# Gate logits in one bank spread by small copies, waits named in a new order, weight loads in paced parts

## The chip, the cores and the metric

One core of a Trainium2 chip. The metric is the device time of one execution in microseconds (us). In these traces PE runs the matmuls (9886 records in the kernel before), ACT the activations (729), DVE and POOL elementwise work (1073 and 626 records), and SP issues 147 of the 151 plain copies. The program gives each engine its own list; where one instruction had to wait, those behind it waited too (POOL in run c1, for 7.0 us).

## The reference, cut to what matters

S = 2048 rows, D = 512, 32 heads of 16. A softmax attention (A) and a linear attention (B) are mixed by a gate per row.

```python
g = sigmoid((x * gate_w).sum(-1, keepdims=True))
a = softmax((q @ k.T) * 16 ** -0.5) @ v @ A_wo            # per head, q, k, v from x @ A_wqkv
b = (phi(q) @ (phi(k).T @ v)) / (phi(q) @ sum(phi(k))) @ B_wo  # q, k, v from x @ B_wqkv
return g * a + (1 - g) * b
```

## The kernel before

A program on the host schedules every instruction of every engine ahead of time. A "round" is one query chunk of 512 rows with half of the heads of one group; there are 32, of about 20 us each. In a round PE makes score blocks. ACT exponentiates pairs of them (695 in all, 128x1024), the path "P". DVE and POOL do the other 658 blocks by integer arithmetic, the path "Z". PE then multiplies both with the values.

Every instruction gets a list of waits on the semaphores of other engines, and they are issued in list order:

```python
    def add(self, fn, deps=(), inc=True, dma_sem=None):
        waits = []
        for d in deps:                       # in the order of the operands
            ...
            for k, (s2, v2) in enumerate(waits):
                if s2 is sem:
                    if val > v2:
                        waits[k] = (sem, val)
                    break
            else:
                waits.append((sem, val))
...
        def emit_engine(E, eng):
            for waits, fn, inc, dma_sem in E.ops:
                for sem, val in waits:
                    eng.wait_ge(sem, val)
                h = fn()
```

The gate's sigmoid is spread over partitions by DVE copies, and each weight matrix is one load:

```python
        def t_gate():
            ...
            for qc in range(NQC):                      # four times: 16 matmuls, a transpose, a copy
                b = yield ("BANK",)
                ... 
                yield dv(607, lambda b=b: nc.vector.transpose(gl, bank(b)), [r_bank[b]], [r_gl])
                yield po(250, lambda qc=qc: nc.gpsimd.tensor_copy(ge[:, qc, :], ...), [r_gl], [r_ge])
            ...                                        # exp on ACT, +1 on POOL, reciprocal on DVE, 1-g on POOL
            for a in range(4):
                yield dv(150, lambda a=a, src=src: nc.vector.tensor_copy(gnat[32 * a:32 * (a + 1), :], src), [r_ge], [r_gnat])
...
        dma(SP, wA[:], wsrc, semWA, 16, 9000.0, writes=[r_wA, r_wAk], issue=500.0)      # 1536 KB
        def t_wb():
            yield ("DMA", wB[:], ..., semWB, 16, 12000.0, [], [r_wB], False, True)      # 1536 KB
```

The queries of each later chunk and group are written as `QT` and copied by eight SP copies into a zero-padded `Qz`, which the scores read:

```python
            for par in range(2):
                for j in range(4):
                    p0 = 32 * j + 16 * par
                    yield ("DMA", Qz[p0:p0 + 16, s, par, :], QT[p0:p0 + 16, a, :], semQ[s], tot, 2500.0, [r_QT[a]], [r_Qz[s][par]], False, j == 0)
```

The softmax here doesn't subtract the row's maximum and nothing guards it: scores larger than these inputs give would overflow.

## Time and profile before

| | before |
|---|---|
| median time of three runs | 681.13 us (680.4 to 681.41) |
| span of the profiled run | 679.8 us |
| ACT's first exponential starts | 10.67 us |
| ACT's last exponential starts | 670.36 us |
| from there to the end | 9.47 us |

ACT is the engine to watch, so I keep one account throughout. The time from one exponential's start to that of ACT's next activation is 904 ns when nothing holds it up, and 477 ns after one of the linear attention's 32 activations; these are the usual shortest steps in the trace. Whatever a step takes beyond them I call **lost**. As the exponentials don't change in number, the span is: start of the first, a fixed floor, the lost time, and the tail after the last. Before, 17.05 us are lost.

ACT's busy time by stretches in the kernel before (columns: stretch, its length, ACT's busy time and instruction count, clock of PE, share of the copy engines, GB/s):

```profile
20.00:40.00 20.00, 13.76 (x15) 0.91 0.45 161
40.00:60.00 20.00, 20.00 (x23) 1.00 0.06 15
60.00:669.00 609.00, 608.43 (x680) 1.00 0.06 15
```

### The profile page before, as it was taken

To read this page: it belongs to the slowest core of one execution; us is meant where nothing else is said; L and a number is where in the kernel's file an instruction comes from. 1 tells how busy PE (TensorE), PEld (TensorE's weight loads), DVE (VectorE), ACT (ScalarE), POOL (GpSimd) and SP (SyncE) were. 2 spreads that over 40 slices of the span, in tenths; PEclk is the share of its full clock that TensorE was granted. 3 is DMA by queue.
4 is the path that set the end of the run, shared out by engine and by line. 5 is a ranking of instruction groups with operands and counts; after the bars stand their busy time and mean duration, and the time that the engine had idled before them with its cause. 6 is when DMAs were issued, how large, how long until landed. Compare 5 with 4: busy or idle time off the path is not lost.

```text
span 679.8 us, 24140 instructions
## 1 busy us (share of the span) xinstructions
PE 664.7 (98%) x9886; PEld 203.6 (30%) x9910; DVE 605.1 (89%) x1073; ACT 658.2 (97%) x734; POOL 550.7 (81%) x626
## 2 busy tenths in 40 slices
PE   8899999999999999999999999999999999999997
PEld 3323232322222222322333322222233322222222
DVE  5789889989899998989899998898999998998995
ACT  5799999999999999999999999999999999999995
POOL 4669878898888888888878888878589888889883
PEclk9999999999999999999999999999999999999999
DMA  6500002100000000000000100000003220000000
GB/s 132 203 18 3 9 2 72 33 2 10 2 9 2 7 6 2 10 2 2 12 3 23 52 10 1 10 3 2 1 11 53 38 49 25 17 18 17 18 18 32
DMA packets 27869, 15.96 MB, mean 23 GB/s; under 512 B 19697, under 2 KB 26737, under 8 KB 27761
## 3 DMA queue, kind: packets, MB, share of 16 engines
q1 hardware_dynamic: 26416, 13.91, 8.0%
q8 instruction: 79, 1.29, 0.8%
q10 hardware_dynamic: 1344, 0.52, 0.3%
q14 instruction: 30, 0.24, 0.1%
HBM read 6.69 MB, written 2.10 MB: 13 GB/s over the span
## 4 chain that ended last, share of the span: by engine, by line
ACT 42%; PE 42%; issue 14%; DVE 1%; DMA 1%; ACTq 0%; POOL 0%; POOLq 0%
ACT P L756 41%; PE ps L363 32%; PE ps L369 9%; ACT eb L1029 1%; DMA xnat<-wA 1%; DVE Z L672 0%; PE ps L884 0%; ACTq L1433 0%; DVE wA L1135 0%; DVE Z L734 0%; DVE T L994 0%; ACT KT L906 0%; ACT wA L1174 0%; POOL warm L407 0%; ACT gt L980 0%
## 5 line engine op out<-in xcount | busy, mean ns | idle before, releaser
L756 ACT ACTIVATE P<-ps 128x1024 bf16<-128x1024 f32 x695 | 645.3, 1126 | 7.4 <-PE ps L363 7.4
L724 POOL TENSOR_TENSOR Z<-Z,mcon 128x512 int32<-128x512 int32 x464 | 477.7, 1054 | 77.6 <-DVE Z L672 46.1
L672 DVE TENSOR_SCALAR Z<-ps 128x512 int16<-128x512 f32 x658 | 441.9, 683 | 57.0 <-PE ps L363 49.8
L363 PE MATMUL ps<-Z,Vc 128*17 128x512 bf16 x1974 | 283.8, 383 | 0.2
L363 PE MATMUL ps<-Qz,KT 32*128 32x512 bf16 x2048 | 272.1, 385 | 4.0 <-ACT P L756 2.3
L363 PE MATMUL ps<-P,Vc 128*17 128x512 bf16 x1390 | 253.0, 383 | 0.0
L363 PEld LDWEIGHTS ps<-Qz,KT 32*128 32x128 bf16 x2048 | 67.9, 91 | 260.4 <-ACT P L756 237.8
L363 PEld LDWEIGHTS ps<-Z,Vc 128*17 128x17 bf16 x1974 | 64.4, 88 | 78.2 <-issue 50.7
L734 DVE TENSOR_SCALAR Z<-Z 128x1024 int16<-128x1024 int16 x194 | 79.8, 430 | 0.2
L363 PEld LDWEIGHTS ps<-P,Vc 128*17 128x17 bf16 x1390 | 57.5, 88 | 55.1 <-issue 42.9
L363 PE MATMUL ps<-warm 128*32 128x512 bf16 (+13 forms) x618 | 59.3, 330 | 4.5 <-issue 3.0
L369 PE MATMUL ps<-xT,wA 128*32 128x512 bf16 x512 | 42.9, 382 | 0.0
L1030 POOL TENSOR_SCALAR eb<-eb 128x512 f32<-128x512 f32 x32 | 19.9, 622 | 16.9 <-DVE Z L734 7.4
L961 POOL TENSOR_SCALAR Vc<-Vc 128x576 bf16<-128x576 bf16 x32 | 21.9, 685 | 8.0 <-DVE Vc L958 5.2
L1017 POOL TENSOR_TENSOR T<-T,rg 128x256 bf16<-128x256 f32 x31 | 19.6, 634 | 8.6 <-DVE Z L734 5.3
L363 PEld LDWEIGHTS ps<-warm 128*32 128x32 bf16 (+1 forms) x642 | 20.8, 95 | 17.5 <-issue 10.3
L994 DVE STREAM_TRANSPOSE T<-ps 128x512 f32<-128x512 f32 x32 | 22.7, 709 | 3.0 <-PE ps L363 2.9
L369 PE MATMUL ps<-wA,xT 128*32 128x128 bf16 x1024 | 22.1, 220 | 2.2 <-issue 2.2
L369 PE MATMUL ps<-wB,xT 128*32 128x512 bf16 x256 | 23.4, 382 | 0.0
L369 PE MATMUL ps<-wA,OAT 128*32 128x512 bf16 x256 | 23.0, 381 | 0.0
L369 PE MATMUL ps<-xT,wB 128*32 128x512 bf16 x256 | 22.4, 383 | 0.0
L369 PE MATMUL ps<-wA,xnat 128*32 128x512 bf16 x256 | 22.3, 381 | 0.0
(79 smaller groups left out, 283.4 us busy)
## 6 DMA issues: line engine op xcount, KB each, us to landing
Qz<-QT SPq DMA_DIRECT2D x120, 16.0 KB, 1.8
wA<-in_A_wqkv_dram SPq DMA_DIRECT2D x1, 1536.0 KB, 7.8
wB<-in_B_wqkv_dram SPq DMA_DIRECT2D x1, 1536.0 KB, 11.9
xnat<-in_A_x_dram SPq DMA_DIRECT2D x3, 512.0 KB, 5.3
out_dram<-outt SPq DMA_DIRECT2D x12, 128.0 KB, 1.7
wA<-in_A_wo_dram SPq DMA_DIRECT2D x1, 512.0 KB, 4.3
wA<-in_B_wo_dram SPq DMA_DIRECT2D x1, 512.0 KB, 5.2
out_dram<-wA SPq DMA_DIRECT2D x4, 128.0 KB, 1.8
```

The lines of the kernel that those rows point to most:

```text
L363: return lambda: nc.tensor.matmul(o, lhsT=l, rhs=r, start=start, stop=stop, skip_group_check=sg)
L369: h = nc.tensor.matmul(o[32 * j:32 * j + 32], lhsT=l[:, 32 * j:32 * j + 32], rhs=r, start=start, stop=stop, skip_group_check=True)
L672: return C(DV, 400, 533 * n + 74, lambda: nc.vector.tensor_scalar(o, i, ZB, 0.0, op0=ALU.add, op1=ALU.max), [r_bank[b] for b in bks], r_Z[ ...
L724: return C(PO, 400, 70 + 484 * n, lambda: nc.gpsimd.tensor_tensor(Z[:, z, 0:512 * n].bitcast(I32), Z[:, z0, 0:512 * n].bitcast(I32), mcon[ ...
L734: return C(DV, 450 if hot else 300, 69 + 134 * n, lambda: nc.vector.tensor_scalar(Z[:, z, 0:512 * n], Z[:, z0, 0:512 * n], float(m), None, ...
L756: return C(AC, 500, 427 * n + 49, lambda: nc.scalar.activation(P[:, slot, 0:512 * n], bank(b0, n), ACT.Exp, scale=ESC), [r_bank[b0 + k] fo ...
L961: yield po(690, lambda k=k: nc.gpsimd.tensor_scalar(Vc[:, k, vs].rearrange("p a b c -> p (a b c)"), Vc[:, 0, vs].rearrange("p a b c -> p ( ...
L994: yield dv(607, lambda: nc.vector.transpose(T1[:, a, :], bank(7)), [r_bank[7]], [r_T1[a]])
L1017: yield po(640, lambda: nc.gpsimd.tensor_tensor(t2[:, :, 16 * par:16 * par + 16], t1[:, :, 0:16], rg[:, a, :].unsqueeze(2).to_broadcast([1 ...
L1029: yield ac(480, lambda: nc.scalar.activation(eb[:, i, :], bank(b), ACT.Exp), [r_bank[b]], [r_eb[i]])
L1030: yield po(640, lambda: nc.gpsimd.tensor_scalar(eb[:, i, :], eb[:, i, :], 1.0 + 1e-6, 0.0, op0=ALU.min, op1=ALU.max), [r_eb[i]], [r_eb[i]])
```

## The change

The intent: let ACT start sooner, keep the heavy loads of the first 40 us apart, relieve DVE and PE of gate work, name the wait that is expected last at the end of the list, and shorten the tail. Besides, 18 instead of 16 buffers for Z and other constants of the scheduler. Cut to its core:

```diff
-        for d in deps:
-            if d is None:
-                continue
+        for d in sorted([d for d in deps if d is not None], key=lambda d: d.fin if isinstance(d, _Ev) else 0.0):
...
                 if s2 is sem:
-                    if val > v2:
-                        waits[k] = (sem, val)
+                    val = max(val, v2)
+                    del waits[k]
                     break
-            else:
-                waits.append((sem, val))
+            waits.append((sem, val))
...
-    FILL = 0.755
+    FILL = 0.7
-    NPS, NZ, NQZ, NVQ = 10, 16, 3, 8
+    NPS, NZ, NQZ, NVQ = 10, 18, 3, 8
...      # gate: logits of all four chunks in one bank, one transpose, one small exp and reciprocal, then
+                for a in range(4):
+                    yield ("DMA", gt[32 * a:32 * (a + 1), qc, :], ge[32 * qc:32 * (qc + 1), 0, :], semGN, 256, 2500.0, [r_ge], [r_gt], False,
+                           qc == 0 and a == 0)
+            yield po(200, lambda: nc.gpsimd.tensor_scalar(gp[:], gt[:].rearrange("p q (c a) -> p a (q c)", a=4), -1.0, 1.0, op0=ALU.mult, op1=ALU.add),
+                     [r_gt], [r_gp])
             for a in range(4):
-                yield dv(150, lambda a=a, src=src: nc.vector.tensor_copy(gnat[32 * a:32 * (a + 1), :], src), [r_ge], [r_gnat])
+                yield ("DMA", gnat[32 * a:32 * (a + 1), :], gp[32 * a:32 * (a + 1), a, :], semGP, 64, 2500.0, [r_gp], [r_gnat], False, a == 0)
...      # loads: each part waits for PE's latest instruction, so PE's progress paces it
+        def t_load(k, n, dst, src, sem, lat, wr, flag):
+            yield ("DMA", dst, src, sem, 16 * n, lat + 1000.0, [now()], wr, False, k == 0)
...
+            add_task(t_load(cc, NCC, wA[:, cc, :], wsrc[:, cc, :], semWA, 3500.0, [r_wA, r_wAk], "wa"), 0.3 + 0.15 * cc, 0.9, f"WA{cc}")
+            add_task(t_load(cc, NCC, wB[:, cc, :], wsrcB[:, cc, :], semWB, 3500.0, [r_wB], "wb"), 0.9 + 0.2 * cc, 1.8, f"WB{cc}")
...      # last round: transpose, reciprocal, products and transpose back in two halves of 256 columns
-            if tail and qbl % 2 == 1:
+            if tail and qbl != 2:
                 yield ac(480, lambda: nc.scalar.copy(ot, bank(b)), [r_bank[b]], [r_ot])
```

## The prediction

> **What bounds the kernel now.** I read the page first: busy shares, the chain of waits, the costliest groups. Two engines are almost full, and the chain is split between them.
>
> ```profile
> PE 664.7 (98%) x9886; PEld 203.6 (30%) x9910; DVE 605.1 (89%) x1073; ACT 658.2 (97%) x734; POOL 550.7 (81%) x626
> ...
> ACT 42%; PE 42%; issue 14%; DVE 1%; DMA 1%; ACTq 0%; POOL 0%; POOLq 0%
> ...
> L756 ACT ACTIVATE P<-ps 128x1024 bf16<-128x1024 f32 x695 | 645.3, 1126 | 7.4 <-PE ps L363 7.4
> L672 DVE TENSOR_SCALAR Z<-ps 128x512 int16<-128x512 f32 x658 | 441.9, 683 | 57.0 <-PE ps L363 49.8
> ```
>
> The kernel divides 2048 score blocks: 1390 are exponentiated in 695 pairs on ACT, 658 by integer arithmetic on DVE and POOL. ACT's own floor decides whether a PE saving can show. I took it from the busy time by stretches, for ACT alone:
>
> ```profile
> 10.60:41.00 30.40, 24.03 (x26) 0.94 0.45 135
> 240.00:320.00 80.00, 80.00 (x89) 1.00 0.02 4
> 545.00:671.00 126.00, 126.00 (x139) 1.00 0.08 21
> ```
>
> From 240 to 320 us ACT runs only exponentials, 80.0/89 = 0.90 us apart, with no idle. Consecutive ones overlap, so the 1126 ns of one is not its price. From 160 to 240 us it runs 85 exponentials and 8 of the phi activations in 80 us, so one of those costs about (80 - 85 x 0.90)/8 = 0.45 us. All of them need 695 x 0.90 + 32 x 0.45 = 640 us. ACT works from its first exponential at 10.7 us to the end of the last at 671.5, which is 661 us. So about 21 us of its window is stretched or idle, 10.7 us precede it and 8.3 us follow it. Only these 40 us can be shortened, because the change keeps 695 exponentials.
>
> The first stretch is the bad one: 6.4 of 30.4 us idle and a clock of 0.94. The timeline of ACT and then PE shows why:
>
> ```profile
> 32.74 1.02 ACT L756 ACTIVATE P<-ps 128x1024 bf16<-128x1024 f32 x1 [3.21 <-PE ps L363]
> 35.62 1.02 ACT L756 ACTIVATE P<-ps 128x1024 bf16<-128x1024 f32 x1 [1.85 <-PE ps L363]
> ...
> 30.89 0.30 PE L369 MATMUL ps<-wA,xT 128*32 128x128 bf16 x4 [2.18 <-issue]
> 31.12 0.61 PE L363 MATMUL ps<-Qz,KT 32*128 32x512 bf16 x2
> ```
>
> PE stops for 2.18 us in the middle of one projection, waiting for nothing it was told to wait for. Afterwards matmuls of 0.39 us take 0.61. The DMA view of 20 to 34 us shows 395 to 424 GB/s until about 28.5 us, from two 1536 KB weight loads issued together, and the view of 28 to 30 us has one instruction packet among them:
>
> ```profile
> wA<-in_A_wqkv_dram SPq DMA_DIRECT2D x1, 1536.0 KB, 7.8
> wB<-in_B_wqkv_dram SPq DMA_DIRECT2D x1, 1536.0 KB, 11.9
> ...
> q8 instruction: 1, 0.02, 3.4%
> ```
>
> [...] ACT pays 3.2 + 1.85 = 5.1 us of idle, 5.4 us with the stretched pitches beside it.
>
> [...] Here the mean clock of 0.94 over 30.4 us is 1.8 us of lost clock, or about 3.6 us at half rate, beginning just after the stall. [...]
>
> **The change part by part.**
>
> *Paced loads.* The two weight loads become eight of 384 KB, each tied to PE's progress, spread over rounds 0.3 to 1.5 instead of back to back at 19 us. A part needs about 1 us at 400 GB/s[...]. Nothing needs wA before about round 0.85 or wB before round 2, and a round is about 20 us. Expected: the 2.18 us stall and the slow clock both go, **-5.4 us**, all on the path.
>
> *Start.* K's first block is projected and copied in halves of 256 columns, so the first scores wait for half a projection and a shorter ACT copy (0.59 us now, about 0.37). Half of the 0.87 us of K matmuls plus 0.22 gives **-0.65 us** on the path.
>
> *Order of the first rounds.* Before, between the 11th and 12th score burst there are 20 waves of other PE work (K, V and a first run of 11 value waves), and ACT loses 1.24 us at about 21 us. The new order still has one such knot, 16 matmuls of K beside value waves and V, a little smaller: **-0.3 us**.
>
> *Gate.* Four groups of 16 matmuls become 16 matmuls in one bank. That is 48/4 x 0.217 = 2.6 us less PE, 3 x 0.70 us fewer DVE transposes, a 0.54 us reciprocal become about 0.24, and four 0.256 us copies become DMAs: about 3.4 us of DVE. Twenty small DMAs are added at about 1.8 us latency (that of the Qz copies), and nothing needs the gate before round 2. Pairing the output reciprocals saves 16 DVE instructions of 0.235 us and 15 POOL ones of 0.23. Most of this lies beside ACT; counted under "middle".
>
> *Wait order, 18 Z slots, other scheduler constants.* The instruction order shows unchanged work: 2048 score, 1974 + 1390 value matmuls, 658 DVE conversions, 695 exponentials. Shifts move slightly, 194 to 199 on DVE and 464 to 459 on POOL. Filler falls from 36.0 to 34.9 us by column count. The score bursts now test DVE first and ACT last, where ACT is the last to arrive in 601 waits. But ACT has another set to work on for 0.90 us while a 0.39 us burst runs, so most late bursts are absorbed. Between 41 and 669 us ACT's stretches of over 60 ns add up to about 6 us; I give the change a third of them, **-2.0 us**.
>
> *Tail.* The last round's DVE chain is now, in sequence:
>
> ```profile
> 672.53 0.72 DVE L994 STREAM_TRANSPOSE T<-ps 128x512 f32<-128x512 f32 x1 [2.54 <-PE ps L363]
> 673.28 0.25 DVE L1001 RECIPROCAL rec<-T 128x16 f32<-128x16 f32 x1
> 673.57 0.17 DVE L1005 TENSOR_TENSOR rg<-rec,gt 128x16 f32<-128x16 f32 x1
> 673.78 0.43 DVE L1006 TENSOR_TENSOR T<-T,rg 128x256 bf16<-128x256 f32 x1
> 674.24 0.71 DVE L1009 STREAM_TRANSPOSE OAT<-T 128x512 bf16<-128x512 bf16 x1
> 675.46 1.29 DVE L1176 CAST wA<-ps 128x512 bf16<-128x512 f32 x2 [0.51 <-PE ps L369]
> ```
>
> It ends at 674.95. I estimate a half at 0.45 + 0.19 + 0.16 + 0.29 + 0.45 = 1.54 us, since each instruction has a fixed part. The first half is ready at 674.1, the second at 675.6: 0.65 us *later* than now. What is won is that two of the four copies and output transfers are out of the way, so the last copy still ends near 676.75 but fewer transfers queue behind it. Net **-0.3 us**.
>
> Sum: 5.4 + 0.65 + 0.3 + 2.0 + 0.3 = 8.65. 681.1 - 8.65 = **672.5 us**.
>
> **Rivals.** (1) *The stall only moves.* If [...]the stall has a cause of its own, the -5.4 falls to between 0 and -2 and the time is 676 to 678. For it: [...]PE resumed about 1 us after the heavy traffic ended.[...] (2) *PE becomes the bound through the clock.* The fill threshold goes from 0.755 to 0.70. [...] Against: total filler hardly falls. (3) *The middle was PE's wait order, not ACT's rate.* Chain: 42% of it is PE. If late score bursts cause most of the 21 us, the new order could recover 6 us more, to about 667. Against: ACT shows no idle from 41 to 480 us and a pitch near its floor. (4) *Small DMAs delay Qz copies on the same queue*: a late query would stall ACT by a few us near round 2, giving 675. Against: queries are made a round ahead.
>
> **Range and chances.** The stall is one visible item with a clear remedy; I give it four chances in five. Without it the time is near 677.5; with it and a better middle, near 668. So 668 to 677.5. Faster by over 2% needs under about 667.7, only with rival 3: 0.08. Slower by over 2% needs several new stalls: 0.01. Within 2%: 0.91.
>
> **What would show it.** In the new profile: no idle over 1 us ended by "issue" on PE between 20 and 40 us; ACT idle from 10 to 41 us near 1.5 us instead of 6.4; clock 1.00 there; first exponential near 10.0 us; an unchanged pitch of 0.90 us in the clean stretch; after the last exponential about 8 us. The prediction is wrong if the clock falls below 1 in later stretches, if ACT's idle reappears elsewhere, or if the middle shortens by far more than 2 us.

-5.4 us rests only on the stop standing beside the loads; that pacing would end it was an estimate. What the trace before does show: half rate from 30.80 to 34.21 us, and no other idle of PE's matmuls by "issue" above 0.3 us. The estimates of DVE's halves use that 128 columns took 284 ns where 512 took 683, and that 0.37 us for ACT's half copy fits 586 ns for 512 columns and 1013 for 1024.

## The result, and the profile after

The change made the kernel slower by 0.8%: 686.33 us (685.86 to 686.49) against 680.88 in the same rounds, ratio 1.0079 with a 95% interval of 1.0061 to 1.0096. Ratios here are the mean time of one kernel's runs over that of the other's in the same rounds, so not quite the ratio of the medians. The account of ACT's time shows where, with four runs from the experiments beside it:

| us | before | after | after, waits reversed | before, waits sorted | best (f1_rev_q_gp) |
|---|---|---|---|---|---|
| span | 679.8 | 684.5 | 679.2 | 682.4 | 673.0 |
| first exponential | 10.67 | 10.00 | 9.77 | 9.92 | 9.87 |
| lost, to 20 | 1.47 | 0.24 | 0.03 | 1.57 | 0.03 |
| lost, 20 to 40 | 5.42 | 3.40 | 2.31 | 3.71 | 2.39 |
| lost, 40 to 60 | 0.12 | 5.76 | 6.63 | 0.42 | 0.31 |
| lost, 60 to 669 | 10.04 | 13.45 | 9.01 | 14.75 | 8.89 |
| tail | 9.47 | 8.84 | 8.84 | 9.38 | 8.83 |

From before to after: -0.67 at the start, -1.23 and -2.02 up to 40 us, then +5.64 between 40 and 60, +3.41 in the long middle, -0.63 in the tail. With 0.14 lost after 669 us that is +4.64, which is what the spans differ by. So most of the early gain came, and two new losses ate it. (The profiled run of f1 is the fastest of its four; the median is given below.) The same stretches of the kernel after:

```profile
20.00:40.00 20.00, 17.41 (x21) 1.00 0.34 102
40.00:60.00 20.00, 14.86 (x16) 0.83 0.25 73
60.00:669.00 609.00, 607.74 (x675) 1.00 0.06 15
```

First row: ACT does 21 instructions instead of 15 and the clock no longer falls. Second row: 16 instead of 23, with a clock of 0.83. Third row: 675 instead of 680, though ACT shows as just as busy.

**The pause at 50 us.** The timelines of PE and ACT after show it (in brackets, the idle time before and what ended it):

```profile
52.70 0.61 PE L377 MATMUL ps<-Qz,KT 32*128 32x512 bf16 x3 [3.31 <-DMA Qz<-QT]
...
53.41 1.02 ACT L779 ACTIVATE P<-ps 128x1024 bf16<-128x1024 f32 x1 [3.38 <-PE ps L377]
```

PE waits for the copies of the next queries. SP's timeline says why they are late:

```profile
34.87 10.75 SPq L358 DMA_DIRECT2D gt<-ge  x16
45.66 5.74 SPq L358 DMA_DIRECT2D Qz<-QT  x8
```

The sixteen gate copies keep SP for 10.75 us, 0.67 us each, though each moves 2 KB; the query copies stand behind them. The eight of those, 16 KB each, take 5.74 us of SP, 0.72 each. From one copy to the next it is usually 0.63 us for both sizes, with one step of 1.28 us among the gate copies and one of 1.36 among the query copies. Little data moves meanwhile: from 36 to 44 us mostly 0 to 4 GB/s, 6 on average. After the pause PE's matmuls take 0.61 us, as after the old one. The clock records show half rate from 51.17 to 58.00 us, 6.83 us; before it was 30.80 to 34.21 us, 3.41 us. Of the 5.76 us lost, 3.5 fall in the step with the pause and 2.1 in the three steps after it, at half rate.

**The long middle.** What PE's weight loads waited for, in the page of all waits (total us, times, longest): before, then after.

```profile
PEld ps L363 <- ACT P L756: 239.9, 601, 0.8
PEld ps L363 <- issue: 116.0, 492, 0.8
...
PEld ps L363 <- DVE Z L672: 13.0, 52, 0.4
```

```profile
PEld ps L377 <- issue: 197.5, 700, 0.6
PEld ps L377 <- ACT P L779: 82.9, 220, 0.6
...
PEld ps L377 <- DVE Z L693: 43.7, 122, 0.8
```

The scores wait for ACT as they did, but much of it is now put down to "issue" and to DVE. The chain of waits changes in the same way, from 42% ACT before to this:

```profile
PE 70%; ACT 21%; issue 4%; DVE 2%; SPq 1%; POOL 0%; DMA 0%; ACTq 0%; DVEq 0%
```

This does not say that PE became the bound by its work: PE is busy 663.0 us after and 664.7 before. The instruction records explain it. In both traces no record of a compute instruction holds more than one wait (before, 1400 of PE's 9910 weight loads hold one, the others none); further waits stand in separate semaphore records ahead of it (578 on PE before, 569 after). I counted this for the first weight load of every score burst, with the time from the end of ACT's exponential to that load (10th percentile and median, over the whole run; smaller groups left out):

```
          separate wait   own wait   bursts   ns from exponential's end
before    none            ACT        485      51, 162
before    DVE             ACT        169      51, 174
after     ACT             DVE        397      113, 199
after     none            ACT        187      78, 201
a1        none            ACT        471      51, 162
a1        DVE             ACT        117      51, 145
```

The one named first stays on the instruction: DVE's in 397 bursts after, ACT's in 117 in a1, which names them the other way round. Sorting so that the last expected is named last therefore puts exactly that one on a separate instruction, and the weight load itself still has DVE's to pass: 113 ns at the 10th percentile instead of 51. With the waits reversed (a1, below) it is 51 again. Bursts without a separate wait came later too, 201 against 162 ns at the median, and the table doesn't say why; with PE's own order alone reversed (g1, below) that median is 156. ACT's exponentials went the same way. Before, the own wait was the one for PE; after, in 612 of some 640 between 60 and 669 us, the wait for PE is separate and the own one is for ACT itself.

**The tail.** DVE's last instructions after (those before are in the prediction):

```profile
677.22 0.45 DVE L1038 STREAM_TRANSPOSE T<-ps 128x256 f32<-128x256 f32 x1 [4.57 <-PE ps L377]
...
680.12 0.45 DVE L1066 STREAM_TRANSPOSE OAT<-T 128x256 bf16<-128x256 bf16 x1
681.07 0.69 DVE L1238 CAST wA<-ps 128x512 bf16<-128x512 f32 x1 [0.51 <-PE ps L383]
```

From the first transpose to the end it is 684.5 - 677.22 = 7.28 us, against 679.8 - 672.53 = 7.27 before. The halves won nothing there; the 0.63 us come from ahead of that transpose.

### The profile page after: what moved, and what is told of

It reads as the page before. It is cut to its first block, busy times and chain, and to the rows that moved or that the text cites. A ratio compares the mean times of both kernels' runs of the same rounds, so it can differ in the third digit from the quotient of the medians.

```text
span 684.5 us, 23841 instructions
## 1 busy us (share of the span) xinstructions
PE 663.0 (97%) x9741; PEld 206.4 (30%) x9777; DVE 604.0 (88%) x1062; ACT 662.2 (97%) x735; POOL 538.7 (79%) x601
## 3 DMA queue, kind: packets, MB, share of 16 engines
q8 instruction: 78, 1.28, 0.8%
## 4 chain that ended last, share of the span: by engine, by line
PE 70%; ACT 21%; issue 4%; DVE 2%; SPq 1%; POOL 0%; DMA 0%; ACTq 0%; DVEq 0%
PE ps L377 55%; ACT P L779 21%; PE ps L383 15%; DVE Z L693 1%; SPq L358 1%; POOL Z L747 0%; DVE T L1042 0%; DMA Qz<-QT 0%; DVE Vc L993 0%; PE ps L907 0%; ACT eb L1090 0%; DVE KT L942 0%; DVE Z L757 0%; PE ps L1009 0%; DVE Qz L959 0%
## 5 line engine op out<-in xcount | busy, mean ns | idle before, releaser
L747 POOL TENSOR_TENSOR Z<-Z,mcon 128x512 int32<-128x512 int32 x459 | 468.9, 1047 | 92.5 <-DVE Z L693 41.7
L377 PE MATMUL ps<-Z,Vc 128*17 128x512 bf16 x1974 | 278.4, 383 | 0.5 <-DVE Z L757 0.3
L377 PE MATMUL ps<-P,Vc 128*17 128x512 bf16 x1390 | 242.4, 384 | 0.3 <-ACT P L779 0.2
L377 PEld LDWEIGHTS ps<-Qz,KT 32*128 32x128 bf16 x2048 | 71.4, 91 | 266.1 <-issue 89.3
L377 PEld LDWEIGHTS ps<-Z,Vc 128*17 128x17 bf16 x1974 | 62.6, 88 | 75.6 <-issue 50.2
L757 DVE TENSOR_SCALAR Z<-Z 128x1024 int16<-128x1024 int16 x199 | 81.5, 428 | 0.0
L377 PEld LDWEIGHTS ps<-P,Vc 128*17 128x17 bf16 x1390 | 54.1, 88 | 59.7 <-issue 46.8
L377 PE MATMUL ps<-warm 128*32 128x512 bf16 (+18 forms) x505 | 53.6, 335 | 5.7 <-issue 4.1
L383 PE MATMUL ps<-xT,wA 128*32 128x512 bf16 (+1 forms) x528 | 43.7, 378 | 0.0
L377 PEld LDWEIGHTS ps<-warm 128*32 128x32 bf16 (+1 forms) x541 | 19.1, 96 | 18.3 <-issue 11.2
```

What stands on the lines that cost most here:

```text
L377: return lambda: nc.tensor.matmul(o, lhsT=l, rhs=r, start=start, stop=stop, skip_group_check=sg)
L383: h = nc.tensor.matmul(o[32 * j:32 * j + 32], lhsT=l[:, 32 * j:32 * j + 32], rhs=r, start=start, stop=stop, skip_group_check=True)
L747: return C(PO, 400, 70 + 484 * n, lambda: nc.gpsimd.tensor_tensor(Z[:, z, 0:512 * n].bitcast(I32), Z[:, z0, 0:512 * n].bitcast(I32), mcon[ ...
L757: return C(DV, 450 if hot else 300, 69 + 134 * n, lambda: nc.vector.tensor_scalar(Z[:, z, 0:512 * n], Z[:, z0, 0:512 * n], float(m), None, ...
```

## The experiments

Two theories. **W**: the order of the waits costs 3 to 5 us in the long middle. **Q**: the sixteen gate copies cost 5 to 6 us at 50 us. Rivals for W: the new scheduler constants, the lower fill threshold or 18 Z buffers cost it, whatever the waits. Rival for Q: the pause would come anyway, from something else. Sixteen kernels were run, three timed rounds each; the kernel before ran beside them at 680.97 to 681.75 us. All outputs are right.

### The order of waits

**a1_waitrev**, the kernel after with the sort reversed:

```diff
-        for d in sorted([...], key=lambda d: d.fin if isinstance(d, _Ev) else 0.0):
+        for d in sorted([...], key=lambda d: d.fin if isinstance(d, _Ev) else 0.0, reverse=True):
...
-                    val = max(val, v2)
-                    del waits[k]
+                    if val > v2:
+                        waits[k] = (sem, val)
                     break
-            waits.append((sem, val))
+            else:
+                waits.append((sem, val))
```

> The changed kernel with its waits sorted the other way round (wait expected last is named first); every instruction and its order are unchanged. Theory W: the build keeps the wait named first on the instruction itself and turns the others into separate semaphore instructions ahead of it, so the change's order put the wait for ACT on the separate instruction; with the reverse the fastest step from the end of an exponential to the scores' weight load falls from 113 to 51 ns, ACT does about 680 instead of 675 instructions between 60 and 669 us, and the time falls by 3 to 4.5 us, to 682 to 683. Rival S: the middle is slower because the new scheduler constants give a worse order of work; then the time stays within 1 us of 686.3.

Measured: 681.04 us (680.76 to 681.17), ratio 0.999 (0.9966 to 1.0014), so 5.3 us better than after, a little more than expected. The loss from 60 to 669 us fell from 13.45 to 9.01; the pause at 50 us stayed.

**b1_waitsort**, the kernel before with only the change's sort:

> The kernel before with nothing but the change's sorting of waits; same instructions in the same order. Theory W: 3 to 5 us slower than before, 684 to 686, with the fastest step from an exponential's end to the scores' weight load at 113 instead of 51 ns in the bursts that wait for two engines. Rival S, or the intent of the change: within 1 us of 681, or faster.

Measured: 685.77 us (683.55 to 687.98), ratio 1.0067 (1.0024 to 1.0109). The loss from 60 to 669 us rose from 10.04 to 14.75. So the order alone does it, in either kernel, and the scheduler's constants aren't needed for it. Its waits look like those of after:

```profile
PEld ps L362 <- issue: 200.9, 707, 0.6
PEld ps L362 <- ACT P L755: 78.1, 203, 0.5
```

**b2_waitrev**, the kernel before with the sort reversed, asks whether the old order lost time too:

> The kernel before with its waits named with the last expected first, the reverse of the change. In it ACT's semaphore already was the own wait of most score weight loads, so little is left: 680.5 (679.5 to 681.5). Under 679 would say that the old order, too, lost time to separate waits.

Measured: 681.14 us, ratio 0.999 (0.9959 to 1.0021). No: before had the late wait in the right place already, by the order in which its operands are listed.

**g1 to g4** reverse the order on some engines of the kernel after only:

```diff
-        for d in sorted([...], key=lambda d: ...):
+        for d in sorted([...], key=lambda d: ..., reverse=(self.name in ("pe",))):   # ("act",), ("pe", "act"), ("dve", "pool")
```

> The changed kernel with only PE's waits in the reverse order, the other four engines' as the change has them. Theory: the loss is the separate wait ahead of PE's score weight load, between an exponential's end and the next scores: 681.3, nearly all of the 5.3 us that reversing every engine's waits gave (681.04). Rival: it is ACT's waits (for PE and for its P buffer) that cost: 685 or more. Half and half: 683.5.

> The changed kernel (686.33 us) with only ACT's waits in the reverse order. With PE's waits alone reversed the loss of about 5.3 us was recovered by a part: 684.03, ratio 1.0035. Theory that the other part is ACT's separate wait ahead of an exponential: 683.5 to 684. Rival, that it is DVE's and POOL's waits: 686, unchanged.

> PE's and ACT's waits reversed, DVE's, POOL's and SP's as the change has them. If PE and ACT hold the whole loss: 681 to 681.7. If DVE and POOL hold the rest: 683.5 or more.

> Only DVE's and POOL's waits reversed. If their separate waits cost only time that those engines have to spare (DVE 75 per cent busy before): 686. If they hold the rest of the loss: 684.

| reversed on | median us | ratio to before | lost, 60 to 669 us |
|---|---|---|---|
| none (after) | 686.33 | 1.0079 | 13.45 |
| PE | 684.03 | 1.0035 | 10.69 |
| ACT | 682.28 | 1.0013 | 10.66 |
| PE and ACT | 681.74 | 1.0011 | 9.19 |
| DVE and POOL | 685.99 | 1.0059 | 13.37 |
| all (a1) | 681.04 | 0.999 | 9.01 |

PE and ACT together hold nearly all of it, DVE and POOL next to nothing. In the traces PE alone and ACT alone each recover 2.8 us of the 4.4, more than half, so the two overlap. I had expected that PE alone would recover nearly everything; it did not. (The 75 per cent for DVE in the last expectation is a slip: the page before has DVE busy 89%.) The medians put ACT above PE, the traces put them level; which weighs more stays open.

### The spread of the gate

**a2_gatelate and a3_both** make the scheduler hold the gate copies back until the second queries are issued, in the kernel after and in a1:

```diff
+            yield ("WAIT", lambda: (0, 1) in Q_ready)
             for qc in range(NQC):
                 for a in range(4):
                     yield ("DMA", gt[...
```

> The changed kernel with its 16 small gate transfers put behind the first eight query copies on the same queue. Theory Q: they held the queue for 10.75 us, so the copies of the second query pair landed at 52.5 us and PE waited 3.3 us for them and then ran at half clock; without it ACT's idle between 40 and 60 us falls from 5.1 us to under 0.5 and the time by 5 to 5.5 us, to 681. Rival P: the paced loads of wB, which wait for PE on the same queue, hold the copies anyway; then the wait for the copies stays above 2 us and the time stays above 684.

> Both edits at once. If theories W and Q are right and act in different stretches their gains add: 686.3 - 3.8 - 5.2 = about 677, which is below the kernel before (681). If one hides the other, 680 or more.

Measured: 686.21 us (ratio 1.0069) and 681.83 us (1.0004): neither gained what was expected. The pause did go; between 40 and 60 us 0.37 and 0.29 us are lost. But the whole schedule moved with that one line. The scheduler left four more blocks of output projections until after the last exponential (156 matmuls of that kind there instead of 80), and the tail grew from 8.84 to 12.24 and 12.26 us. A condition in a scheduler is not a local edit. For the rest I moved instructions after scheduling, so that all else keeps its order.

**c1_rev_qfirst and c2_qfirst** put the eight query copies ahead of the sixteen gate copies in SP's list, in a1 and in the kernel after:

```diff
+        gi = [k for k, o in enumerate(SP.ops) if o[3] is semGN]        # the 16 gate copies
+        qi = list(range(gi[-1] + 1, gi[-1] + 9))                       # the 8 query copies behind them
+        SP.ops = SP.ops[:gi[0]] + [SP.ops[k] for k in qi] + [SP.ops[k] for k in gi] + SP.ops[qi[-1] + 1:]
```

> The changed kernel with the waits reversed and, after scheduling, the eight copies of the second query pair moved ahead of the 16 gate transfers on the queue of SP; no other engine's instruction moves (the earlier try, which delayed the gate in the scheduler, also moved four of the final projections behind the last exponential and gave its gain back there). Theory Q: the stall of 4.4 us at 47 us and the 2.1 us of half clock after it go, so 681.0 - 6 = 675, ACT's stretch from 40 to 60 us under 0.6 us, tail 8.8 us as before. Rival P (paced loads hold the queue): 679 or more.

> The changed kernel with only the move on the queue of SP, waits as the change has them. Theory Q: 686.3 - 5.5 = 680.8. With c1 and a1 this closes the square: if the two causes are independent, each edit is worth the same with and without the other, within 1 us. Rival P: 685 or more.

Measured: 681.29 us (0.9999) and 686.16 us (1.0075): no gain. Theory Q, as I had it, was not enough. The waits of c1 from 44 to 62 us show a new one:

```profile
POOL gp L1026 <- DMA gt<-ge: 7.0, 1, 7.0
ACT P L780 <- PE ps L378: 6.0, 2, 5.1
...
PE ps L378 <- POOL Z L748: 4.9, 1, 4.9
```

POOL's list holds up what stands behind, too. Its operation that reads the gate (`gp`) waits 7.0 us for the copies, the Z shifts behind it stand still, PE waits 4.9 us for a shift and ACT 5.1 for PE. There were two waits beside each other, and the second took over when the first was removed.

**f1_rev_q_gp and f2_q_gp** move that operation of POOL as well, to just ahead of the first one that uses the gate, about ten microseconds later, and the four copies that read it behind the next query copies (values in the waits adjusted to the new order):

```diff
+        PO.ops = PO.ops[:k0] + PO.ops[k0 + 1:k1] + [PO.ops[k0]] + PO.ops[k1:]              # k0: gp, k1: first rg
+        SP.ops[g0:g0 + 4 + ng] = SP.ops[g0 + 4:g0 + 4 + ng] + SP.ops[g0:g0 + 4]            # g0: gnat copies
```

> The changed kernel with its waits in the reverse order and the second pair's query copies ahead of the 16 gate copies (that combination alone ran 681.29 us), and now the operation of POOL that reads the spread gate moved some ten microseconds later in POOL's own order, behind the shifts it held back, with the four small copies that need it moved behind the next query copies. Theory of two queues in order: the pause of about 5 us at 50 us was POOL waiting 7.0 us for the gate copies, so it goes: ACT's excess in 40 to 60 us falls from 6.5 us to under 1.5, and the time to 675.5 (674.5 to 677.5), faster than both kernels. Rival, that something else stops there next (DVE's shifts, score clock, a fetch): under 2 us are gained and a new named wait stands at 50 us. Rival, that the gain is given back later, as it was when the scheduler was made to delay the gate: the pause goes, the last exponential starts at 665 and the stretch after it grows.

> The same two moves with the change's own order of waits (this without POOL's move ran 686.16 us). If the order of waits and the spread of the gate are independent and add up: 680.5 (679.5 to 682.5), some 5 us above the run with reversed waits. If they overlap, the gap to that run is under 3 us.

Measured: **676.02 us** (674.67 to 679.14), ratio 0.9936 (0.9896 to 0.9975), and 679.99 us, ratio 0.998 (0.9953 to 1.0007). Both times were as expected. f1 beats both kernels. Its ACT stretches, and the operation of POOL, which now waits for nothing:

```profile
20.00:40.00 20.00, 18.38 (x22) 1.00 0.36 107
40.00:60.00 20.00, 20.00 (x23) 1.00 0.23 68
...
58.11 0.30 POOL L1026 TENSOR_SCALAR gp<-gt 128x64 f32<-128x64 f32 x1
```

The two causes nearly add. From 686.33, reversing the waits gives 5.3 us, freeing both queues 6.3, both together 10.3 by the medians; by the ratios, which compare within the same rounds, 6.1, 6.7 and 9.7. From f2 to f1 that is 4.0 us or 3.0, not quite the 5 that I had expected.

### The paced loads

**d1_unpaced and f3_unpaced** release all eight parts at once, in c1 and in f1:

```diff
+        # after scheduling: the 8 parts of wA and wB keep their place ahead, without their waits for PE
+        SP.ops = SP.ops[:li[0]] + [([],) + tuple(SP.ops[k][1:]) for k in li] + rest
```

> c1 with the eight weight loads issued in a row at about 19 us, without waiting for PE; all else in the same order. Theory F (fetch): [...]a gap of PE with nothing awaited of 1.5 to 2.5 us returns between 24 and 31 us, with a slow clock after it, and the time is 3 to 5 us above c1. Rival: the stall before came from something else; then within 1 us of c1.

(The theory's gap and the time it expects rest on the stop in the kernel before.)

> The best run so far (676.02 us: waits reversed, query copies first, POOL's gate operation moved) with the eight parts of the two weight loads released at once instead of paced. If the paced loads are worth what the prediction gave them once the later stall is gone: 681.4 (5.4 us more). If what they save is partly absorbed elsewhere, as the earlier test beside a later stall had it: 679.8 (3.8 us more). A stall of 2 to 4 us by issue on PE and half clock after it should stand between 25 and 40 us.

Measured: d1 685.07 us (ratio 1.0058), 3.8 us above c1; f3 678.59 us (0.9958), 2.6 us above f1 by the medians and 1.5 by the ratios. From f1 to f3 the span grows 2.8 us and the loss from 20 to 40 us from 2.39 to 5.58, so pacing is real, if less than either figure that I had expected for f3. Single profiles vary here: over the five without pacing (before, b1, b2, d1, f3) the loss from 20 to 40 us is 3.71 to 8.45, mean 5.9; over the thirteen with it 2.31 to 3.66, mean 2.9. That puts pacing near 3 us by the traces (1.5 to 4.0 by the times and ratios of the two pairs), not 5.4. PE's stop is back in f3:

```profile
30.55 0.41 PE L384 MATMUL ps<-wA,xT 128*32 128x128 bf16 x16 [1.78 <-issue]
```

The stop's place is a hint at its cause. The page lists q8 as a queue of instructions: 79 packets of 16 KB before and 78 after, one for every 255.7 and 255.0 of PE's records on average, so I take them for PE's. In all five traces without pacing PE stops after 959 to 962 records, though the lists of d1 and f3 are others than those of before, b1 and b2, and goes on 1.3 to 1.6 us after the end of a packet (before: packet from 28.48 to 29.56 us, PE again at 30.89). PE had come to record 898 to 959 when that packet began; in the thirteen with pacing to 768 to 836, and none of them has the stop. That PE lacked instructions because a packet came late beside the loads is my reading of these places; no record names what ended the stop, and which packets of the loads held anything up is not shown.

What the stop costs depends on the clock. It fell to half rate with the stops of 1.57 (b2), 2.18 (before) and 3.14 us (d1), but not with those of 1.74 (b1) and 1.78 us (f3), with granted clocks of 0.997, 0.997 and 0.990 over the run against 1.000 and 0.999; at the pause in the kernel after it fell 1.78 us after PE's last matmul. So the length of a stop alone does not tell whether the clock falls. In f3 the stop costs 1.75 us; another 1.2 us more than in f1 goes at 21.7 us, where PE waits 1.34 us for POOL's `Vc`, so not all of the 3 us is the stop.

In f1 ACT still loses 2.4 us in that stretch, 1.68 of them in two steps at 20.7 and 22.1 us, ahead of the place of the old stall.

### The tail in halves

**e1_whole** is c1 with the last round's output whole and the old share of the tail copies:

```diff
-                yield tr_half(0)        # and the loop over two halves
+            yield dv(607, lambda: nc.vector.transpose(T1[:, a, :], bank(7)), [r_bank[7]], [r_T1[a]])
-            if tail and qbl != 2:
+            if tail and qbl % 2 == 1:
```

> c1 with the last round in one piece, as in the kernel before, and its copies two and two. Reading of the traces: from the first transpose of the last round to the end it was 7.27 us before and 7.28 after, so the halves win nothing: within 0.4 us of c1. The intent of the change: 0.5 us or more slower than c1.

Measured: 681.56 us (0.9994 to 1.0026) against c1's 681.29; tails 8.97 and 8.84 us. The halves are worth 0.1 to 0.3 us at most, within the spread of the runs.

## Why the prediction was wrong, point by point

- **Start, -0.65: right.** The first exponential starts 0.67 us sooner in the two profiles, at the predicted 10.00. The bare start moves by more than that between runs (9.58 to 10.67 us with the old start); ACT's copy of the transposed inputs already starts anywhere from 5.78 us (b2) to 6.71 (before). So I also took it from that copy: 3.96, 3.97 and 3.80 us in before, b1 and b2; 3.42 and 3.29 in after and f1.
- **Paced loads, -5.4, and the first knot, -0.3: the stop went as predicted, size too large.** (A detail of the reading: the clock fell at 30.80 us, 2.1 us into the stop of 2.18, not after it.) The row "20 to 40" and the clock behaved as listed: the longest stop by "issue" on PE there is 0.80 us, the clock is 1.00. But ACT's loss up to 40 us fell by 3.25 us, and in f1, without the wait order's share, by 4.47. The step that failed is the assumption that all idle after the stall goes with it: from 20 to 40 us some 2.9 us stay lost with pacing, and about 3 us is what pacing takes away, part of it a wait for POOL and not the stop.
- **Wait order in the middle, -2.0: wrong in sign.** The step was "the score bursts now test DVE first and ACT last", taken as a gain of a third of the small losses. I had not asked which of several waits stays on the instruction. By the records it is the one named first. In its place PE and ACT each passed a separate wait late, and the order alone costs 4.4 to 4.7 us by the traces and some 5 by the times (a1, b1). Without it the middle shows 9.01, about 1 us better than before; whether the 18 Z buffers or the other constants earned that was not tested.
- **Gate, nothing on the path: wrong, the largest term.** The step was "nothing needs the gate before round 2". True of the gate's readers, and beside the point: the copies hold SP (10.75 us), and the operation that waits for them holds POOL (7.0 us in c1). That cost 5.64 us between 40 and 60 us, shown by f1 and f2. **Rival 4** named the right mechanism, "small DMAs delay Qz copies on the same queue", with 675 us; I dismissed it because queries are made a round ahead. That holds for when they are computed, not for when their copy gets its turn. I also priced a gate copy by its latency of 1.8 us and not by the 0.67 us that SP needs to issue it, sixteen times.
- **Tail, -0.3: too small, for another reason.** It gained 0.63, but not by the halves (e1).
- **Rivals 1 to 3** do not decide it. The stall did not simply move (1): what stands at 50 us has another cause. The clock of 1.00 after 60 us speaks against (2); the prediction's own sign of being wrong, a clock below 1 in a later stretch, came at 50 us, but from the pause. Of (3) the sensitivity was right, several us in the middle hang on PE's waits, but the sign was not.

Together: the prediction's sum was -8.65 us. With both new losses removed, f1 is 5.7 us below before by the medians of the same rounds and 4.4 by the ratio (1.7 to 7.1); only its profiled run, the fastest, is 6.9 below by the span. So the rest of the change is worth half to four fifths of what it promised.

## What to carry to other kernels

A copy has a place in the issuing engine's order and an operation that waits for it has one in its own; before sending small copies through a queue, add up what each costs to issue (here 0.67 us for 2 KB) and look at what stands behind both. Where an instruction waits on several engines, find out from the trace which wait stays on the instruction, and try giving that place to the one that arrives last on the critical loop (here 51 ns from an exponential's end to the weight load instead of 113, at the 10th percentile, and some 5 us of the whole). When one wait is removed and the time does not move, look for the next engine that waits for the same event before dropping the theory.
